# A gated decode block on one core: w_o's last part in 8 steps around the last value block, and the joining of one head's output moved into the middle of that block's products

## Chip, cores and metric

The kernel runs on one core of one Trainium2 chip. The metric is device microseconds (us) of one execution, and the figure compared is the median of several executions. One execution was also taken by the hardware profiler; its trace gives the span from the first to the last instruction and every duration used below.

## What is computed

Two rows of 448 numbers, `x`, are normalised, passed through attention against a cache of 4096 keys for 2 batches and 8 key/value heads of width 256 (two query heads share each), projected back by `w_o`, multiplied by a gate and added to `x`. The gate is a bilinear feed-forward block under a SiLU. All is float32.

```python
xn = _layernorm(x)
q = (xn @ wq).reshape(B, 1, 16, 256)
scores = einsum("bhqd,bhkd->bhqk", q, k) * 256 ** -0.5
o = einsum("bhqk,bhkd->bhqd", softmax(scores), v)
s = o.reshape(B, 1, 4096) @ wo          # wo: 4096 x 448
g = silu(((xn @ w_gate) * (xn @ w_up)) @ w_down)
return x + s * g
```

## The kernel before: tiling, stages and what sets their order

Nearly all the work is reading: keys and values are 16 blocks each (8 heads by 2 batches) of 128 partitions by 8192 floats (4096 KB by the profile), and every weight is laid out in the same shape. All these tiles come through one pool, `ring`, of five buffers. The function `plan` (line 51) writes the order of the transfers by hand, and `issue` (line 54) hands the next one to SyncE's DMA queue (SPq in the profile); a transfer may be cut by columns into several DMAs, so that its first part can be used before its last has landed. A transfer waits until the last reader of the tile five places earlier in that order is done.

The order of the last transfers (lines 76 to 81) is: the second part of `w_o` ("wo1", 10 steps), the keys of block 14, the keys of block 15, the values of block 14, the values of block 15 (four DMAs of 4096, 2048, 1024 and 1024 columns) and the last part of `w_o` ("wo2", 6 steps, as three DMAs of 3, 2 and 1 steps). A **step** of `w_o` is one of its 32 slices of 128 rows by 448 columns, 224 KB. Four steps belong to each head; steps 28 to 31 are the last head's.

The program is scheduled by hand: each engine runs its instructions in the order of the code.

- `scores` (line 194) makes 16 matmuls of keys against the queries (line 204) and two row maxima on VectorE (DVE, line 205).
- `softmax` (line 209) joins the maxima through small matmuls (lines 212 and 217), takes the exponentials on ScalarE (ACT, line 223), transposes them (line 225) and sums them (line 228).
- `values` (line 232) makes 16 matmuls with the values (line 238), accumulating in a PSUM bank `o` of which there is one, and then evacuates it through ScalarE into `ob`, with the softmax's division (line 240). The 16 products of one block use its columns in order, 512 each.
- `combine` (line 242) joins the pieces of a block's output by 8 small matmuls (line 248) in bank `cb`; `turn` (line 257) transposes the result on VectorE (line 258) into the form in which it meets `w_o`.
- `project` (line 263) multiplies steps of `w_o` at full width into bank `wide`; `spread` (line 161) moves that bank through ScalarE into bank `acc` (lines 164 and 166), and `project_last` (line 269) adds the remaining steps straight into `acc`, four matmuls of 112 columns each (line 272).

Blocks 0 to 13 run one after the other (lines 281 to 304), each with its scores, softmax and values. Then the outputs of six of them are joined, 10 steps of `w_o` are projected and spread, the scores and softmax of blocks 14 and 15 run, and then comes the tail that the change rewrites (lines 316 to 326): values of 14, joining of 14, values of 15, steps 26 and 27, joining of 15, steps 28 to 31. At the end two VectorE instructions multiply by the gate and add `x` (lines 330 and 331) and SyncE writes the result (line 332).

Of the kernel before, what the change touches and what calls it, by code (L numbers as in the profile page):

```python
# [9 lines left out]
AF = mybir.ActivationFunctionType  # L10
# [3 lines left out]
B, D = 2, 448  # L14
HKV, REP, SK, DH = 8, 2, 4096, 256
# [6 lines left out]
KB = 16  # L22
ROW = 8192
SL = D // NT
NC = HKV * 4
EARLY = 16
LATE = 26
EPS = 1e-5


# [5 lines left out]
def gated_decode_block(ctx: ExitStack, tc: tile.TileContext, x, xo, kt, v, wq, wo, wg, wu, wd, out):  # L36
    nc = tc.nc
# [6 lines left out]
    def bank(name="s", bufs=3):  # L44
        return psum.tile([128, 512], F32, name=name, bufs=bufs)
# [5 lines left out]
    def plan(name, src, cuts=None):  # L51
        todo.append((name, src, cuts or [0, src.shape[1]]))

    def issue(n=1):
        for name, src, cuts in todo[:n]:
            t = loaded[name] = ring.tile([128, ROW], F32, name="ring", align_bytes=512)
            for lo, hi in zip(cuts, cuts[1:]):
                nc.sync.dma_start(t[:, lo:hi], src[:, lo:hi])
        del todo[:n]

    N = HKV * B
    LAST = N - B
    plan("wq0", wq[0])
    for i in range(LAST):
# [10 lines left out]
        plan(f"v{i}", v[i % B, i // B])  # L75
    plan("wo1", wo[:, EARLY * D:LATE * D])
    plan(f"k{LAST}", kt[0, HKV - 1])
    plan(f"k{LAST + 1}", kt[1, HKV - 1])
    plan(f"v{LAST}", v[0, HKV - 1])
    plan(f"v{LAST + 1}", v[1, HKV - 1], [0, 4096, 6144, 7168, 8192])  # L80
    plan("wo2", wo[:, LATE * D:], [0, 3 * D, 5 * D, 6 * D])
    issue(5)

    x2 = const.tile([B, D], F32)
# [65 lines left out]
    def query(h):  # L150
        ps = bank()
        rows(ps, loaded[f"wq{h}"], 512)
        for r in range(REP):
            nc.vector.transpose(qT[h][:, :, :, :, r, :].rearrange("p b g d j -> p (g d) b j"),  # L154
                                ps[:, r * 256:(r + 1) * 256])
# [13 lines left out]
    def ffn_in():  # L169
        pp = []  # L170
        for w in ("wg", "wu"):
            ps = bank()
            rows(ps, loaded[w], FC)
            pp.append(ps)
        g = work.tile([128, FC], F32, name="h")
        nc.scalar.copy(g, pp[0][:, :FC])
        h = work.tile([128, FC], F32, name="h")
        nc.vector.tensor_mul(h, pp[1][:, :FC], g)
        nc.vector.transpose(hT.rearrange("p i m -> p (i m)"), h)

    def ffn_out():
        ps = bank()
        for i in range(14):
            t = i % NT
            nc.tensor.matmul(ps[W * t:W * (t + 1), :D], hT[:, i], loaded["wd"][:, i * D:(i + 1) * D],  # L185
                             start=i < NT, stop=i >= 14 - NT)
        y = bank()
        spread(ps, y, True, True)
        e = const.tile([128, SL], F32)
        nc.scalar.activation(e, y[:, :SL], AF.Sigmoid)  # L190
        nc.vector.tensor_mul(gate, y[:, :SL], e)


    def scores(i):
        g, b = divmod(i, B)
        k = loaded[f"k{i}"].rearrange("p (h d c n) -> p h d c n", h=2, d=2, c=NT)
        q = qT[g // 4][:, b, g % 4].rearrange("p d r j -> p d (r j)")
        m = work.tile([128, 4], F32, name="m")
        ss = []
        for h in range(2):  # L200
            s = bank()
            for d in range(2):
                for c in range(NT):
                    nc.tensor.matmul(s[W * c:W * (c + 1), :], q[:, d], k[:, h, d, c, :], start=d == 0, stop=d == 1)  # L204
            nc.vector.tensor_reduce(m[:, h:h + 1], s, axis=AX.X, op=OP.max)  # L205
            ss.append(s)
        return ss, m

    def softmax(ss, m):
        nc.vector.tensor_max(m[:, 2:3], m[:, 0:1], m[:, 1:2])  # L210
        sm = bank("sm", 1)
        nc.tensor.transpose(sm[:1, :128], m[:, 2:3], ident)  # L212
        mx = work.tile([1, NT, W], F32, name="mx")
        nc.vector.tensor_reduce(  # L214
            mx, sm[:1, None, :128].rearrange("p o (c j) -> p o j c", c=NT).to_broadcast([1, NT, W, NT]),
            axis=AX.X, op=OP.max)
        nc.tensor.matmul(sm[:, 128:129], mx.rearrange("p c j -> p (c j)"), one, start=True, stop=True)  # L217
        nc.vector.tensor_scalar(m[:, 3:4], sm[:, 128:129], -1.0 / 16, None, op0=OP.mult)  # L218
        su = work.tile([128, 4], F32, name="su")
        pT = []  # L220
        for h in range(2):
            p = work.tile([128, 512], F32, name="p")
            nc.scalar.activation(p, ss[h], AF.Exp, bias=m[:, 3:4], scale=1.0 / 16, accum_out=su[:, h:h + 1])  # L223
            t = work.tile([128, KB, W], F32, name="pT", bufs=4)
            nc.vector.transpose(t.rearrange("p i m -> p (i m)"), p)  # L225
            pT.append(t)
        nc.vector.tensor_add(su[:, 2:3], su[:, 0:1], su[:, 1:2])  # L227
        nc.tensor.matmul(sm[:, 130:131], add_head.rearrange("p a r j -> p (a r j)"), su[:, 2:3], start=True, stop=True)  # L228
        nc.vector.reciprocal(su[:, 3:4], sm[:, 130:131])
        return pT, su[:, 3:4]  # L230

    def values(i, pT, ob):

        pT, r = pT
        o = bank("o", 1)
        for e in range(KB):
            h, t, at = e // 8, e % NT, e % 8 * 2 * W
            nc.tensor.matmul(o[W * t:W * (t + 1), :], pT[h].rearrange("p i m -> p (i m)")[:, at:at + 2 * W:2],  # L238
                             loaded[f"v{i}"][:, e * 512:(e + 1) * 512], start=e < NT, stop=e >= KB - NT)
        nc.scalar.activation(ob, o, AF.Copy, scale=r)  # L240

    def combine(ob, n):

        cb = bank("cb", 1)
        src = ob.rearrange("p s (e d c k) -> p s e d c k", e=2, d=2, c=NT)
        for e in range(2):
            for c in range(NT):
                nc.tensor.matmul(cb[W * c:W * (c + 1), :n * 64], add_blocks[:, e].rearrange("p r j -> p (r j)"),  # L248
                                 src[:, :n, e, :, c, :], start=e == 0, stop=e == 1)
        return cb  # L250


    wide = bank("wide", 1)
# [3 lines left out]
    def turn(oT, cb, g, b, n):  # L257
        nc.vector.transpose(oT[:, g:g + n, :, :, DUP * b:DUP * (b + 1)].rearrange("p g d r j -> p (g d) r j"), cb)  # L258

    def heads(oT, i, first):  # L260
        return oT[:, i // 4 - first, i % 2, i % 4 // 2]

    def project(oT, first, lo, hi, name, base):
        for i in range(lo, hi):
            t = i % NT
            nc.tensor.matmul(wide[W * t:W * (t + 1), :D], heads(oT, i, first),  # L266
                             loaded[name][:, (i - base) * D:(i - base + 1) * D], start=i < NT, stop=i >= LATE - NT)

    def project_last(oT, first, i):
        for n in range(NT):  # L270
            at = (i - LATE) * D + n * SL
            nc.tensor.matmul(acc[W * n:W * (n + 1), :SL], heads(oT, i, first), loaded["wo2"][:, at:at + SL],  # L272
                             start=False, stop=i == NC - 1)

    query(0)
    issue()
    ob = work.tile([128, 8, 512], F32, name="ob", bufs=1)
    oT0 = const.tile([128, 4, 2, REP, W], F32)
    oT1 = const.tile([128, 3, 2, REP, W], F32)
    oT2 = const.tile([128, 1, 2, REP, W], F32)  # L280
    for i in range(LAST):
        g, b = divmod(i, B)
        ss = scores(i)
        issue()
        p = softmax(*ss)
        values(i, p, ob[:, b * 4 + g if g < 4 else b * 3 + g - 4])
        issue()
        if i == 1:
            ffn_in()
            issue(2)  # L290
        if i == 2:
            ffn_out()
            issue()
        if i == 5:
            query(1)
            issue()
        if i == 7:
            cb = combine(ob, 8)
            for n in range(B):
                turn(oT0, cb[:, n * 256:(n + 1) * 256], 0, n, 4)  # L300
            ob = work.tile([128, 8, 512], F32, name="ob", bufs=1)
        if i == 8:
            project(oT0, 0, 0, EARLY, "wo0", 0)
            issue()
    cb = combine(ob, 6)
    for n in range(B):
        turn(oT1, cb[:, n * 192:(n + 1) * 192], 0, n, 3)
    project(oT1, 4, EARLY, LATE, "wo1", EARLY)
    issue()
    spread(wide, acc, True, False)  # L310
    ps = []
    for i in range(LAST, N):
        ss = scores(i)
        issue()
        ps.append(softmax(*ss))
    for i in range(LAST, N):
        b = i - LAST
        values(i, ps[b], ob[:, 6 + b])
        issue()
        if b == B - 1:  # L320
            for n in range(LATE, NC - 4):
                project_last(oT1, 4, n)
        cb = combine(ob[:, 6 + b:], 1)
        turn(oT2, cb[:, :64], 0, b, 1)
    for i in range(NC - 4, NC):
        project_last(oT2, 7, i)

    r0 = const.tile([128, SL], F32)
    r1 = const.tile([128, SL], F32)
# [40 lines left out]
```

## Time and profile before

| what | value |
|---|---|
| median of 3 runs | 380.46 us (379.8 to 380.95) |
| profiled execution | 379.4 us, of which the span is 377.3 us |
| TensorE matmul (PE) | busy 221.4 us, 59% |
| TensorE weight load (PEld) | busy 64.9 us, 17% |
| VectorE / ScalarE | busy 72.7 us / 39.8 us |
| bytes moved by DMA | 158.75 MB, mean 421 GB/s |
| mean granted TensorE clock | 0.78 of full |

How to read it: the span is cut into stages with different limits, so the busy shares of the whole do not tell what the end waits for. Three views matter here. The chain of waits follows the last instruction back to what released it. The windows view gives, for any stretch, how long each engine was busy, which share of the TensorE clock was granted (PEclk) and what the DMA engines moved. The list of DMA issues gives, for each transfer, its size and the time from issue to landing. A matmul of this kernel appears as two records in the trace, so the 16 matmuls of `values` are 32 records, and one step in `project_last` is 8.

### The profile page before, as it was taken

What the parts mean: (1) busy time and instruction counts of PE and PEld (TensorE: products, weight loads), DVE (VectorE), ACT (ScalarE), POOL (GpSimd) and SP (SyncE); (2) the same over time, 40 slices, a digit from 0 to 9 for tenths busy, and PEclk for the clock granted to TensorE, in tenths of its full rate; (3) what the DMA queues carried; (4) which work ended last, traced back from release to release, by engine and by line L of the source; (5) the groups of instructions that cost most, each with busy time, mean ns of one, the idle gap of its engine ahead of it and who ended that gap; (6) DMA issues with size and microseconds to landing.
All of it is one profiled execution on the core that took longest, in us unless ns stands there. A gap on an engine that the chain in (4) does not pass through costs nothing.

```text
span 377.3 us, 3373 instructions
## 1 busy us (share of the span) xinstructions
PE 221.4 (59%) x1444; PEld 64.9 (17%) x1444; DVE 72.7 (19%) x176; ACT 39.8 (11%) x87; POOL 1.2 (0%) x7
## 2 busy tenths in 40 slices
PE   0665565667365556546566655664656476575765
PEld 0112121112111211101122111121112121111122
DVE  3013120121021402102121310213021210304211
ACT  1001011002202100100102100021002010111020
POOL 1000000000000000000000000000000000000000
PEclk9966968666966878887876877669786966699668
DMA  8999999999999999999999999999999999999992
GB/s 338 437 434 419 431 438 434 419 438 449 427 419 438 438 436 431 423 434 441 433 424 429 433 442 438 417 436 434 440 424 431 438 429 445 424 432 436 410 419 94
DMA packets 6530, 158.75 MB, mean 421 GB/s; under 512 B 754, under 2 KB 884, under 8 KB 1396
## 3 DMA queue, kind: packets, MB, share of 16 engines
q1 hardware_dynamic: 6496, 158.54, 97.8%
q8 instruction: 11, 0.18, 0.2%
q14 instruction: 3, 0.02, 0.0%
q10 hardware_dynamic: 20, 0.01, 0.0%
HBM read 158.54 MB, written 0.00 MB: 420 GB/s over the span
## 4 chain that ended last, share of the span: by engine, by line
DMA 72%; PE 21%; DVE 4%; issue 1%; ACT 1%; SPq 0%; ACTq 0%
DMA ring<-kt 60%; DMA ring<-v 12%; PE s L204 10%; PE o L238 8%; DVE pT L225 1%; PE s L185 1%; PE cb L248 1%; DVE m L205 1%; DVE mx L214 1%; PE sm L228 1%; ACT ob L240 1%; PE sm L217 0%; ACT p L223 0%; PE sm L212 0%; PE acc L272 0%
## 5 line engine op out<-in xcount | busy, mean ns | idle before, releaser
L204 PE MATMUL s<-ring,qT 128*32 128x512 f32 x512 | 80.6, 786 | 51.2 <-DMA ring<-kt 51.1
L238 PE MATMUL o<-ring,pT 128*32 128x512 f32 x512 | 85.5, 830 | 2.0 <-DMA ring<-v 2.0
L205 DVE TENSOR_REDUCE m<-s 128x1 f32<-128x512 f32 x32 | 22.1, 692 | 175.4 <-PE s L204 175.4
L223 ACT ACTIVATE p<-s,m 128x512 f32<-128x512 f32 x32 | 21.7, 682 | 196.8 <-DVE m L218 196.7
L204 PEld LDWEIGHTS s<-ring,qT 128*32 128x32 f32 x512 | 20.1, 138 | 109.6 <-issue 78.3
L228 PE MATMUL sm<-su,add_head 128*128 128x1 f32 x32 | 9.1, 353 | 42.5 <-DVE su L227 42.5
L238 PEld LDWEIGHTS o<-ring,pT 128*32 128x32 f32 x512 | 20.1, 147 | 52.9 <-issue 52.4
L225 DVE STREAM_TRANSPOSE pT<-p 128x512 f32<-128x512 f32 x32 | 22.1, 711 | 15.7 <-ACT p L223 15.7
L142 PE MATMUL s<-ring,xnT 128*32 128x512 f32 (+1 forms) x96 | 14.9, 772 | 13.2 <-DMA ring<-wq 8.4
L240 ACT ACTIVATE ob<-o,su 128x512 f32<-128x512 f32 x16 | 11.0, 687 | 109.4 <-PE o L238 109.4
L228 PEld LDWEIGHTS sm<-su,add_head 128*128 128x128 f32 x32 | 7.7, 300 | 43.8 <-DVE su L227 43.8
L212 PE MATMUL sm<-ident,m 128*1 128x128 f32 x16 | 4.3, 269 | 17.3 <-DVE m L210 17.3
L217 PE MATMUL sm<-one,mx 1*128 1x1 f32 x32 | 6.5, 270 | 12.4 <-DVE mx L214 12.4
L214 DVE TENSOR_REDUCE mx<-sm 1x128 f32<-1x512 f32 x16 | 10.9, 679 | 7.0 <-PE sm L212 7.0
L266 PE MATMUL wide<-ring,oT 128*32 128x448 f32 x52 | 7.4, 686 | 4.1 <-DMA ring<-wo 3.4
L217 PEld LDWEIGHTS sm<-one,mx 1*128 1x128 f32 x32 | 5.1, 199 | 15.8 <-DVE mx L214 15.8
L142 PEld LDWEIGHTS s<-ring,xnT 128*32 128x32 f32 x96 | 3.6, 137 | 23.0 <-issue 18.1
L258 DVE STREAM_TRANSPOSE oT<-cb 128x256 f32<-128x256 f32 (+2 forms) x6 | 1.9, 346 | 26.5 <-PE cb L248 26.5
L212 PEld LDWEIGHTS sm<-ident,m 128*1 128x1 f32 x16 | 1.3, 79 | 32.0 <-issue 26.1
L223 ACT ACTIVATION_READ_ACCUMULATOR p<-s,m 128x1 f32 x32 | 6.3, 196 | 0.0
L248 PE MATMUL cb<-ob,add_blocks 128*32 128x64 f32 (+2 forms) x64 | 4.3, 385 | 2.9 <-ACT ob L240 2.9
L154 DVE STREAM_TRANSPOSE qT<-s 128x256 f32<-128x256 f32 x4 | 1.6, 428 | 22.3 <-PE s L145 22.3
(53 smaller groups left out, 40.3 us busy)
## 6 DMA issues: line engine op xcount, KB each, us to landing
ring<-kt SPq DMA_DIRECT2D x16, 4096.0 KB, 40.7
ring<-v SPq DMA_DIRECT2D x15, 4096.0 KB, 41.9
ring<-wq SPq DMA_DIRECT2D x2, 3584.0 KB, 11.4
ring<-wo SPq DMA_DIRECT2D x1, 3584.0 KB, 40.8
ring<-wg SPq DMA_DIRECT2D x1, 3136.0 KB
ring<-wu SPq DMA_DIRECT2D x1, 3136.0 KB
ring<-wd SPq DMA_DIRECT2D x1, 3136.0 KB, 35.1
ring<-wo SPq DMA_DIRECT2D x1, 2240.0 KB, 37.9
```

Source lines behind the costliest of these rows:

```text
L142: nc.tensor.matmul(ps[W * c:W * (c + 1), :n], xnT[:, k, :], block(NT * k + c), start=k == 0, stop=False)
L204: nc.tensor.matmul(s[W * c:W * (c + 1), :], q[:, d], k[:, h, d, c, :], start=d == 0, stop=d == 1)
L205: nc.vector.tensor_reduce(m[:, h:h + 1], s, axis=AX.X, op=OP.max)
L214: nc.vector.tensor_reduce(mx, sm[:1, None, :128].rearrange("p o (c j) -> p o j c", c=NT).to_broadcast([1, NT, W, NT]), axis=AX.X, op=OP.max)
L217: nc.tensor.matmul(sm[:, 128:129], mx.rearrange("p c j -> p (c j)"), one, start=True, stop=True)
L223: nc.scalar.activation(p, ss[h], AF.Exp, bias=m[:, 3:4], scale=1.0 / 16, accum_out=su[:, h:h + 1])
L225: nc.vector.transpose(t.rearrange("p i m -> p (i m)"), p)
L228: nc.tensor.matmul(sm[:, 130:131], add_head.rearrange("p a r j -> p (a r j)"), su[:, 2:3], start=True, stop=True)
L238: nc.tensor.matmul(o[W * t:W * (t + 1), :], pT[h].rearrange("p i m -> p (i m)")[:, at:at + 2 * W:2], loaded[f"v{i}"][:, e * 512:(e + 1) * ...
L240: nc.scalar.activation(ob, o, AF.Copy, scale=r)
L248: nc.tensor.matmul(cb[W * c:W * (c + 1), :n * 64], add_blocks[:, e].rearrange("p r j -> p (r j)"), src[:, :n, e, :, c, :], start=e == 0, s ...
L266: nc.tensor.matmul(wide[W * t:W * (t + 1), :D], heads(oT, i, first), loaded[name][:, (i - base) * D:(i - base + 1) * D], start=i < NT, sto ...
```

## The change

The second part of `w_o` has 8 steps instead of 10 and the last part 8 instead of 6. The last part is laid out in memory in another order, 24, 25, 28, 29, 30, 31, 26, 27, and fetched by four DMAs of 2, 4, 1 and 1 steps. The values of block 15 come in three DMAs (4096, 3072 and 1024 columns) instead of four. Block 15's products are accumulated in bank `wide`, which `spread` has emptied by then, instead of in `o`. The first 8 of them stand ahead of the joining of block 14, the other 8 behind it. Step 24 stands where steps 26 and 27 stood (ahead of the joining of 15), step 25 behind that joining, then steps 28 to 31, and steps 26 and 27 last.

```diff
-LATE = 26
+LATE = 24
+THIRD = [24, 25, 28, 29, 30, 31, 26, 27]
...
-    plan(f"v{LAST + 1}", v[1, HKV - 1], [0, 4096, 6144, 7168, 8192])
-    plan("wo2", wo[:, LATE * D:], [0, 3 * D, 5 * D, 6 * D])
+    plan(f"v{LAST + 1}", v[1, HKV - 1], [0, 4096, 7168, 8192])
+    plan("wo2", wo[:, LATE * D:], [0, 2 * D, 6 * D, 7 * D, 8 * D])
...
-    def values(i, pT, ob):
-
-        pT, r = pT
-        o = bank("o", 1)
-        for e in range(KB):
+    def values(i, pT, o, lo=0, hi=KB):
+
+        for e in range(lo, hi):
...
-        nc.scalar.activation(ob, o, AF.Copy, scale=r)
...
     def project_last(oT, first, i):
         for n in range(NT):
-            at = (i - LATE) * D + n * SL
+            at = THIRD.index(i) * D + n * SL
             nc.tensor.matmul(acc[W * n:W * (n + 1), :SL], heads(oT, i, first), loaded["wo2"][:, at:at + SL],
-                             start=False, stop=i == NC - 1)
+                             start=False, stop=i == THIRD[-1])
...
-        values(i, p, ob[:, b * 4 + g if g < 4 else b * 3 + g - 4])
+        o = bank("o", 1)
+        values(i, p[0], o)
+        nc.scalar.activation(ob[:, b * 4 + g if g < 4 else b * 3 + g - 4], o, AF.Copy, scale=p[1])
...
-    for i in range(LAST, N):
-        b = i - LAST
-        values(i, ps[b], ob[:, 6 + b])
-        issue()
-        if b == B - 1:
-            for n in range(LATE, NC - 4):
-                project_last(oT1, 4, n)
-        cb = combine(ob[:, 6 + b:], 1)
-        turn(oT2, cb[:, :64], 0, b, 1)
-    for i in range(NC - 4, NC):
+
+    o = bank("o", 1)
+    values(LAST, ps[0][0], o)
+    nc.scalar.activation(ob[:, 6], o, AF.Copy, scale=ps[0][1])
+    issue()
+    o = bank("wide", 1)
+    values(LAST + 1, ps[1][0], o, 0, KB // 2)
+    cb = combine(ob[:, 6:], 1)
+    turn(oT2, cb[:, :64], 0, 0, 1)
+    values(LAST + 1, ps[1][0], o, KB // 2, KB)
+    nc.scalar.activation(ob[:, 7], o, AF.Copy, scale=ps[1][1])
+    project_last(oT1, 4, 24)
+    cb = combine(ob[:, 7:], 1)
+    turn(oT2, cb[:, :64], 0, 1, 1)
+    project_last(oT1, 4, 25)
+    for i in range(28, 32):
         project_last(oT2, 7, i)
+    for i in range(26, 28):
+        project_last(oT1, 4, i)
...
-    wo = c(np.asarray(A_wo).reshape(NC, 128, D).transpose(1, 0, 2)).reshape(128, NC * D)
+    wo = np.asarray(A_wo).reshape(NC, 128, D)[[*range(LATE), *THIRD]]
+    wo = c(wo.transpose(1, 0, 2)).reshape(128, NC * D)
```

## The prediction

> **What bounds the kernel now.** I read the DMA row of the page first, then the chain of waits backwards from the end, then the windows view of the tail, then the DMA issues.
>
> ```profile
> DMA  8999999999999999999999999999999999999992
> DMA 72%; PE 21%; DVE 4%; issue 1%; ACT 1%; SPq 0%; ACTq 0%
> ```
>
> The DMA engines are full until the last of 40 slices. No edit changes the bytes, so everything up to the last landings stays, and only the tail can move. The chain's last pieces (start, us, what):
>
> ```profile
> 311.12 38.42 DMA ring<-kt
> ...
> 349.59 6.19 PE s L204 x32
> ...
> 361.46 5.34 PE o L238 x32
> ...
> 366.83 0.70 ACT ob L240
> ...
> 367.57 0.43 PE cb L248 x16
> 368.00 3.48 PE o L238 x32
> ...
> 371.50 0.70 ACT ob L240
> ...
> 372.24 0.47 PE cb L248 x16
> ...
> 372.74 0.26 DVE oT L258
> ...
> 373.04 1.02 PE acc L272 x32
> ```
>
> So behind the landing of block 15's keys at 349.55 nothing waits for a transfer any more: TensorE and what it hands to ScalarE and VectorE set the end. The last steps of `w_o`, by the DMA issues (KB, us to landing):
>
> ```profile
> ring<-wo SPq DMA_DIRECT2D x1, 448.0 KB, 32.1
> ring<-wo SPq DMA_DIRECT2D x1, 224.0 KB, 22.6
> ```
>
> The timeline has the last of them issued at 349.56, so it landed at 372.2; the last 1024 columns of V (issued 333.85, 35.1 us) landed at 368.95. The six steps took 3.25 us, 0.54 each. The final 32 records start 0.84 us after the last landing: that, and the 1.02 us of those records, is all the room there is in front of the transfers.
>
> TensorE's clock decides the pace. In windows of 3.41 us (PE busy, records, PEclk, DMA share, GB/s):
>
> ```profile
> 351.25:354.67 3.42, 3.42 (x20) 0.50 0.89 383
> 354.67:358.08 3.41, 1.53 (x15) 1.00 1.01 432
> 358.08:361.49 3.41, 0.83 (x8) 0.50 0.93 399
> 361.49:364.91 3.42, 3.42 (x20) 0.50 1.00 420
> 364.91:368.32 3.41, 2.59 (x44) 1.00 1.02 419
> ```
>
> The granted clock is 1.00 or 0.50 and changes only at multiples of 3.41 us from one another, all through the trace. Half became full after a window busy 3.13 us, not after one of 2.97; full became half after 1.53, not after 1.65. A record of 512 columns takes 0.107 us of pace at full clock and 0.213 at half (rows of four: 0.43 and 0.85).
>
> **The change, part by part.**
>
> *Two steps later in the queue.* 2 x 0.54 = 1.08 us of transfer move behind the last V, so both last keys and values land 1.08 earlier; block 15's keys at 348.47. TensorE can use it: the project ahead has 16 records instead of 20 (2.45 us down to 1.96), so scores of 14 start about 1.0 earlier, and that block's last small matmul ends at 347.87 (before 348.87), ahead of the keys. Block 15's values land whole at 367.87 and, at 0.54 us per 224 KB, their first 2048 KB at 362.9; block 14's, 4096 KB or 9.9 us ahead of that, by 358.1. None is late below.
>
> What the 1.08 brings depends on the window grid. **On the profiled grid**: scores of 15 run at half clock to 354.67. Before, (354.67 - 349.59) / 0.213 = 23.8 of 32 records, and 8.2 x 0.107 = 0.88 behind; now 28.9, and 0.33 behind: 0.55 earlier, half of the shift. The softmax chain is fixed. Values of 14 start at 360.9, at half clock to 364.91: 18.8 records, then 13.2 x 0.107 = 1.41 instead of 1.69. Of 1.08, **0.28** is left. **Over all positions of the grid** nothing is lost: work and grid shifted together give the same durations, so the mean gain is about 1.0 to 1.08.
>
> *Half of the last V's products ahead of the joining of 14.* Before, TensorE idles 0.82 us at 366.75 (its idle time before L248), waiting for ScalarE's 0.70 evacuation. Now 16 records (1.71 us at full clock) stand there in another bank: **-0.82**. Queued behind the joining are the other 16 products, which need ScalarE at 367.5, long done at 368.2. If block 15's values were late, the cover would go and 0.82 come back; the first half lands 3 us ahead. The joining itself (0.24 us until the next products start) stays.
>
> *Order of the steps.* Step 24 (8 records, about 0.25) hides under the evacuation of 15 (0.70), where 26 and 27 were hidden; step 25 under the transpose (0.26). Behind the transpose stand 48 records instead of 32: 1.02 x 1.5 = 1.53, **+0.51**. What is queued behind step 24 is the joining of 15; its step lands at 367.87 + 1.08 = 368.95 and is asked for at 370.2. Steps 28 to 31 land by 371.1, 26 at 371.7, 27 at 372.2 again.
>
> *DMAs.* V has one piece less, w_o one more; SP still issues seven in the same order, all over 20 us before their landing, past waits that end about 1 us earlier. DVE's and ACT's orders hold as many instructions as before. I price this at nothing, with 0.1 either way; the cover is the queue's backlog.
>
> **Sum.** On the profiled grid -0.28 - 0.82 + 0.51 = -0.59: the accumulation ends at 373.5 instead of 374.06, 1.3 behind the last landing, and what follows (two VectorE instructions, the write) stays. 379.4 becomes 378.8. With the shift in full: -1.04 - 0.82 + 0.51 = -1.35. The floor is the last landing and one step, 372.20 + 0.25 + about 0.2 (a record of `acc` lasts 0.26 us at a pace of 0.03): 372.65, 1.41 below the profiled end.
>
> Which grid do the runs have? The three lie 0.4 to 1.55 us above the profiled one, though the transfers are the same; a step to full clock that comes 1 us later costs 0.5 us in each of the two stages above, so 1 or 2 us give that much. On the profiled grid block 14's products meet the change to full 3.5 us after their start, and since a window must be busy 3.13 us, hardly a grid is kinder to that stage. So the typical run has a later step and gains more than 0.59. The Trainium skill, "TensorE: Matmul & The Clock Gate", "Part 1: The HAM clock gate", says that the activity window is 3413 ns, free-running, and is not reset when a kernel starts. The trace agrees with 3.41 us, and that the grid's place differs by execution one profile cannot show; by that rule the sum would be -1.35, with a fixed grid -0.59.
>
> I take -1.25, the full shift less a little that the floor takes where TensorE is early anyway. From the median: 380.46 - 1.25 = **379.2 us**. A measurement of this kernel can tell about 0.3%, 1.14 us, from no change.
>
> **Rivals.**
>
> 1. *The grid is the same in every execution.* For it: one profile, one grid. Against it: runs that spread over 1.15 us. Then -0.59: 379.9. Chance 0.25.
> 2. *The floor is reached in the typical run.* If a window that was just not busy enough (347.84 to 351.25 holds 2.25 us; with work 1.08 earlier about 2.9 of the needed 3.13) counts, the clock rises one window earlier, and the end falls to the last landing. From a median run 1.06 above the profiled one that is -(1.06 + 1.41) = -2.5: 378.0. For: how close 2.9 is to 3.13. Against: it needs it in most grids. Chance 0.15.
> 3. *Nothing is there to gain.* Where the clock rises early in both kernels, both end at the floor, and the 0.51 behind the transpose is paid without the 0.82 saved: 0 to +0.2, 380.6. For: then products of 15 wait for V in both. Against: the chain shows no such wait. Chance 0.12.
> 4. *Slower: TensorE overtakes the transfers and loses its clock.* Place: the window in which the last products wait for V. Products of a block need 3.45 us at full clock and its values 9.7 us to land, so a TensorE that has caught up is busy 35% of the time, under the 1.65 of 3.41 (48%) that kept the clock. Then the 48 last records run at half: between nothing and 1.53 more, with the last products and the joining another 0.7. From the profiled end -0.59 + 2.2 = +1.6; 382.1 from the median. It decides when the window around 368.3 to 371.7 holds under 1.65 us of work; on the profiled grid it holds over 2.5 in the new order (8 products, the joining, a step), so I give it 0.08.
>
> **Numbers.** The forecast has 0.40. Faster by over 0.3% means under 379.3: most of rival 2, a bit over half of the forecast's spread and a little of rival 1: 0.47. Within: the rest of those two and rival 3: 0.45. Slower: rival 4 in full, 0.08. The range leaves out rival 4 and the outer halves of 2 and 3: 378.0 to 380.5.
>
> **What would show it.** Block 15's keys landing near 348.5; no idle of 0.8 us before the first small joining; the last 48 records starting about 1 us before the old 373.0 and ending at 372.7 to 373.5; the last landing within 0.2 us of 372.2. I am wrong if TensorE waits for a landing of `w_o` ahead of the joining of 15, if PEclk is 0.50 behind 368, or if the last landing moves.

## The result and the profile after

| | median | runs |
|---|---|---|
| before | 380.57 us | 379.8 to 381.35, 6 runs |
| changed | 378.26 us | 377.87 to 378.55, 6 runs |

The ratio is 0.994, 95% interval 0.9924 to 0.9956: 2.3 us faster, by 1.7 to 2.9. The forecast was 1.25 us faster, 379.2: the time lies inside the forecast's range, but 1.25 lies outside this interval. A second measurement (e6 below) gave 0.9958, 0.9942 to 0.9975, which is 1.6 us, by 1.0 to 2.2. The changed kernel's runs lie within 0.7 us of one another; those of before, over all measurements here, from 378.73 to 381.54. The profiled execution of the changed kernel, 378.55 us with a span of 376.4, is the slowest of its six; that of before, 379.4, was faster than all six of its runs.

The page: the DMA engines are as full as before, and their part of the chain grew from 72% to 76% while TensorE's fell from 21% to 18%.

```profile
DMA  8999999999999999999999999999999999999993
DMA 76%; PE 18%; DVE 3%; issue 1%; ACT 1%; SPq 0%; ACTq 0%
```

The chain's end in the changed kernel (start, us, what), to be laid beside the one in the prediction:

```profile
311.03 37.77 DMA ring<-kt
...
348.84 6.54 PE s L205 x32
...
361.02 5.49 PE o L237 x32
366.50 1.72 PE wide L237 x16
368.22 0.22 PE cb L246 x16
368.44 1.77 PE wide L237 x16
...
370.24 0.69 ACT ob L326
...
370.98 0.47 PE cb L246 x16
...
371.48 0.26 DVE oT L256
...
371.78 1.40 PE acc L270 x48
```

ScalarE's evacuation of block 14, which stood between the two blocks' products at 366.83, is gone from the chain: the first 16 records of block 15 stand in its place, and the joining follows without a gap. Block 15's keys land at 348.80 (before 349.55), its products end 1.3 us earlier, the accumulation ends at 373.18 (before 374.06). The last landing is at 372.57 (issued 348.81, 23.8 us), before 372.2.

The window grid of this profile is almost that of before (PE busy, records, PEclk, DMA share, GB/s; the first line is from the profile of before, the others from this one):

```profile
347.84:351.25 3.41, 2.25 (x10) 0.50 1.02 442
...
347.80:351.21 3.41, 2.95 (x14) 0.50 0.94 404
351.21:354.62 3.41, 3.41 (x20) 0.50 1.01 437
...
361.45:364.86 3.41, 3.41 (x20) 0.50 1.00 421
364.86:368.28 3.42, 3.42 (x52) 1.00 1.01 418
```

So the two profiles can be laid on one another: both rise to full clock at 354.6 and at 364.9. On this one grid the accumulation ended 0.88 us earlier, of which 0.85 shows in the time (379.4 to 378.55). The rest of the 2.3 lies in where the two profiled executions stand among the runs: that of before 1.17 us below its median, that of the changed kernel 0.29 above.

### The profile page after: what moved, and what is told of

It is laid out like the page before. It is cut to its first block, busy times and chain, and to the rows that moved or that the text cites. A ratio compares the mean times of both kernels' runs of the same rounds, so it can differ in the third digit from the quotient of the medians.

```text
span 376.4 us, 3397 instructions
## 1 busy us (share of the span) xinstructions
PE 222.5 (59%) x1456; PEld 65.6 (17%) x1456; DVE 72.7 (19%) x176; ACT 39.8 (11%) x87; POOL 1.2 (0%) x7
## 4 chain that ended last, share of the span: by engine, by line
DMA 76%; PE 18%; DVE 3%; issue 1%; ACT 1%; SPq 0%; ACTq 0%
DMA ring<-kt 55%; DMA ring<-v 12%; DMA ring<-wd 9%; PE s L205 8%; PE o L237 6%; DVE pT L226 1%; PE wide L237 1%; PE s L186 1%; PE cb L246 1%; DVE m L206 1%; DVE mx L215 1%; PE sm L229 0%; PE acc L270 0%; SPq L59 0%; PE sm L218 0%
## 5 line engine op out<-in xcount | busy, mean ns | idle before, releaser
L205 PE MATMUL s<-ring,qT 128*32 128x512 f32 x512 | 82.0, 799 | 50.9 <-DMA ring<-kt 50.9
L237 PE MATMUL o<-ring,pT 128*32 128x512 f32 x480 | 82.4, 849 | 1.6 <-DMA ring<-v 1.6
L237 PEld LDWEIGHTS o<-ring,pT 128*32 128x32 f32 x480 | 18.9, 149 | 51.5 <-issue 50.9
L286 ACT ACTIVATE ob<-o,su 128x512 f32<-128x512 f32 x14 | 9.6, 687 | 98.8 <-PE o L237 98.8
L264 PE MATMUL wide<-ring,oT 128*32 128x448 f32 x48 | 6.6, 698 | 4.1 <-DMA ring<-wo 3.3
```

Source lines behind the costliest of these rows:

```text
L286: nc.scalar.activation(ob[:, b * 4 + g if g < 4 else b * 3 + g - 4], o, AF.Copy, scale=p[1])
```

## The experiments

All were compared with the kernel before on the same chip. "Theory A" is what I held after the first result: TensorE's chain behind block 15's keys sets the end, each part of the change takes time from it, and the places of the clock's steps make the spread.

**e1, the split alone.** The kernel before with the products of block 15 in bank `wide`, 8 on each side of the joining; nothing else.

```diff
...
+    o = bank("wide", 1)
+    values(LAST + 1, ps[1][0], o, 0, KB // 2)
+    cb = combine(ob[:, 6:], 1)
+    turn(oT2, cb[:, :64], 0, 0, 1)
+    values(LAST + 1, ps[1][0], o, KB // 2, KB)
...
```

> The kernel before with one part of the change: block 15's products go to the bank wide, 8 of them stand ahead of the joining of block 14 and 8 behind it; the transfers, their cuts and the order of w_o's steps are those of before. Theory A (the end is set by TensorE's chain behind the landing of block 15's keys, every part of the change takes time from that chain, and the place of the clock's steps adds the spread): the 0.8 us of idle ahead of the first small joining is gone, nothing is added behind the transpose, so about 0.8 below before, 379.6 to 379.9, and a spread over 1 us as before. Rival B (the two steps moved behind the last V are all of the gain): within 0.3 of before. Rival C (the idle is all of it): within 0.4 of the changed kernel, 378.3 to 378.7.

Measured: 379.61 against 380.21; ratio 0.9985, 0.9968 to 1.0003, so 0.6 us, between 1.2 and nothing: A's size, but not clear of zero. Runs from 378.24 to 380.83. The profiled one was the slowest, and its timeline shows why (start, us, records, idle time before and what ended it):

```profile
340.50 5.20 PE L204 MATMUL s<-ring,qT 128*32 128x512 f32 x32 [2.00 <-DMA ring<-kt]
...
350.81 0.59 PE L228 MATMUL sm<-su,add_head 128*128 128x1 f32 x2 [2.58 <-DVE su L227]
351.33 1.08 PE L204 MATMUL s<-ring,qT 128*32 128x512 f32 x4
```

On this grid the project of `w_o` had run at full clock, TensorE then waited 2.00 us for block 14's keys, and the window 336.87 to 340.28 held only 1.00 us of work. The clock fell, the scores of block **14** took 5.20 us instead of 3.64, its softmax ended at 351.4, and the keys of block 15, landed at 350.12, waited 1.2 us for TensorE. In the profile of before those scores met full clock:

```profile
339.55 3.64 PE L204 MATMUL s<-ring,qT 128*32 128x512 f32 x32 [0.52 <-DMA ring<-kt]
```

**e2, the split undone.** The changed kernel with all of block 15's products behind the joining of 14.

```diff
-    values(LAST + 1, ps[1][0], o, 0, KB // 2)
     cb = combine(ob[:, 6:], 1)
     turn(oT2, cb[:, :64], 0, 0, 1)
-    values(LAST + 1, ps[1][0], o, KB // 2, KB)
+    values(LAST + 1, ps[1][0], o)
```

> The changed kernel with the split undone: all 16 products of block 15 stand behind the joining of block 14 again; the transfers and the order of the steps are the changed ones. Theory A: the idle of 0.8 us comes back, so 0.7 to 0.9 above the changed kernel, 379.0 to 379.2, and the profile's accumulation ends about 1.4 us behind the last landing instead of 0.6. Rival B: as the changed kernel, 378.3. Rival C: as before, 380.5.

Measured: 378.81 against 380.21; 0.9962, 0.9948 to 0.9976, so 1.45 us faster than before, and 0.55 above the changed kernel's first median, where theory A had 0.7 to 0.9. The idle time is back in the timeline; the second line is that of the kernel before:

```profile
366.39 0.42 PE L246 MATMUL cb<-ob,add_blocks 128*32 128x64 f32 x15 [0.82 <-ACT ob L319]
...
367.57 0.43 PE L248 MATMUL cb<-ob,add_blocks 128*32 128x64 f32 x16 [0.82 <-ACT ob L240]
```

The accumulation ends 1.10 us behind the last landing (372.12), where theory A had about 1.4. Rival C (the split is all) does not hold: most of the gain is there without it. Rival B (the shift is all) is not excluded by the ratios, 0.9962 here against 0.994 and 0.9958 (e6) for the changed kernel, whose intervals overlap. Against it speaks that ten of e2's twelve runs lie above 378.55, the highest of the changed kernel's twelve, though those were measured apart from these.

**e3 and e4, both kernels with TensorE kept busy: a fill that was too big.** 17 extra matmuls in the gaps of each of the last two softmax chains; their result is read by nobody.

```diff
+    def warm(n):
+        d = bank("cb", 1)
+        for _ in range(n):
+            nc.tensor.matmul(d[:W, :D], add_tiles.rearrange("p b j -> p (b j)"),
+                             hT.rearrange("p i m -> p (i m)"), start=True, stop=True)
...
+        if fill[0]:
+            warm(fill[0])
         nc.tensor.transpose(sm[:1, :128], m[:, 2:3], ident)
...
-        ps.append(softmax(*ss))
+        ps.append(softmax(*ss, (4, 3, 10)))
```

> The changed kernel with 17 extra matmuls of 448 columns whose result nobody reads, in the gaps of each of the last two softmax chains (4, 3 and 10 ahead of their three small matmuls), which keep TensorE busy while it would wait. Theory A, with the clock as the cause of the spread: scores of block 15 and values of block 14 run at full clock on every place of the window grid, both end 2 to 3 us earlier, the end is left to the last landing, and all runs lie within 0.4 of 377.9. Rival D (a TensorE that overtakes the transfers loses its clock again in the last windows): PEclk 0.50 behind 365 us, the 48 last records up to 1.5 us longer, 378.3 to 379.5. Rival E (the clock is not what bounds): as the changed kernel, 378.3, with its spread of 0.7.

> The kernel before with the same 17 extra matmuls in the gaps of each of the last two softmax chains. Theory A: with the clock full TensorE is early enough in the old order too, so the end is left to the last landing and the change is worth under 0.4: 377.8 to 378.3, against 380.5 without the fill. Rival E (the clock is not what bounds): as before, 380.5. Between (order and clock both count): 378.6 to 379.6, with the idle ahead of the small joining still 0.8 us.

Measured: 390.67 and 391.86, ratios 1.0267 and 1.0315: 10 and 12 us slower, which none of the theories had. The error was the size of the fill:

```profile
348.49 7.70 PE L213 MATMUL cb<-hT,add_tiles 128*32 128x448 f32 x20
```

Twenty records of 448 columns took 7.70 us, 0.385 each, where 512 columns in `values` are paced at 0.107. All of the fill writes one group of 32 rows of the bank; the 16 matmuls of `values` go round four groups. So the fill held back both softmax chains by several us. The clock was full in every window, so these runs say what a fill costs and nothing on the theories.

**e6, the changed kernel again**, beside the next three on one chip.

> The changed kernel once more, for its spread and for another place of the window grid, beside the next three on one chip. Theory A (the shifted transfers let TensorE reach the last landing on nearly every grid): median 0.9 to 1.2 below the kernel with the split undone relative to the kernel before, that is 1.8 to 2.3 below before, and a spread under 1.2 us where before has over 2. Rival: the 2.3 of the first measurement was a matter of grids, then 0.6 to 1.2.

Measured: 378.14 (377.82 to 378.55) against 379.85 (379.12 to 380.87); 0.9958, 0.9942 to 0.9975. The 1.6 us fall between theory A (1.8 to 2.3) and its rival (0.6 to 1.2), and against e2's ratio the split brings 0.15 us here, where A had 0.9 to 1.2; only the small spread, 0.7, came as A said. The grid of this profile stands 0.3 us later than in the first, and on it TensorE was early. Block 15's keys landed at 348.32, the window behind them was nearly filled, and the clock rose at its end, one window earlier than the 354.6 of the first two profiles:

```profile
348.10:351.52 3.42, 3.15 (x16) 0.50 1.06 460
351.52:354.93 3.41, 2.29 (x21) 1.00 0.92 399
...
371.04 0.97 PE L270 MATMUL acc<-ring,oT 128*32 128x112 f32 x32 [0.18 <-DVE oT L256]
372.21 0.94 PE L270 MATMUL acc<-ring,oT 128*32 128x112 f32 x16 [0.20 <-DMA ring<-wo]
```

The four steps of the last head are done at 372.0, and then TensorE waits for `w_o`: step 26, and step 27, whose landing is at 372.7 (issued 348.34, 24.4 us). The accumulation ends 0.44 us behind that. This is the floor, and 378.55, the highest of these six runs, was its profile: the last landing was 0.5 later than in the trace of before.

**e7, the shift alone.** `w_o`'s steps in their natural order, no split; the last part has 8 steps. The lines are against the changed kernel; block 15's products stand as in e2.

```diff
-THIRD = [24, 25, 28, 29, 30, 31, 26, 27]
+THIRD = [24, 25, 26, 27, 28, 29, 30, 31]
...
-    plan("wo2", wo[:, LATE * D:], [0, 2 * D, 6 * D, 7 * D, 8 * D])
+    plan("wo2", wo[:, LATE * D:], [0, 4 * D, 6 * D, 7 * D, 8 * D])
...
-    project_last(oT1, 4, 24)
+    for i in range(24, 28):
+        project_last(oT1, 4, i)
```

> The shift alone: w_o's last part has 8 steps, in the natural order 24 to 31, fetched by DMAs of 4, 2, 1 and 1; steps 24 to 27 stand ahead of the joining of block 15 and 28 to 31 behind its transpose, as 26 and 27 and 28 to 31 did before; block 15's products are not split. Theory A as the prediction has it: -1.0 to -1.1 against before, 0.3 to 0.5 better than without the split but with the new order. Rival F (the shift is worth more than it moves, because on some grids block 14's scores also start at half clock and block 15's keys then wait for TensorE): -1.4 to -1.9. Rival G (the shift is lost at half clock as on the first profile's grid): -0.3.

Measured: 378.58 (377.99 to 380.35); 0.9968, 0.9954 to 0.9982, so 1.2 us below before, by 0.7 to 1.75. That is the prediction's full shift; rival G (0.3) is out, F (1.4 to 1.9) can't be told from it. Against e2, which has the new order besides, it is 0.2 us slower by the ratio, though 0.2 lower by the median: a cost of the new order is too small for these times to tell. In this profile too the clock rose one window early, after one that held 2.86 us:

```profile
347.99:351.40 3.41, 2.86 (x17) 0.50 0.99 423
351.40:354.81 3.41, 2.30 (x22) 1.00 0.95 408
```

**e8 and e9, the light fill.** 8 matmuls of 224 columns in each of the two chains, sized by e3 (the lines are against e3 and e4).

```diff
-            nc.tensor.matmul(d[:W, :D], add_tiles.rearrange("p b j -> p (b j)"),
-                             hT.rearrange("p i m -> p (i m)"), start=True, stop=True)
+            nc.tensor.matmul(d[:W, :D // 2], add_tiles.rearrange("p b j -> p (b j)"),
+                             hT[:, :7].rearrange("p i m -> p (i m)"), start=True, stop=True)
...
-        ps.append(softmax(*ss, (4, 3, 10)))
+        ps.append(softmax(*ss, (2, 1, 5)))
```

> The changed kernel with 8 extra matmuls of 224 columns, whose result nobody reads, in each of the last two softmax chains (2, 1 and 5 ahead of the three small matmuls), sized by the first fill: a record on one column group took 0.385 us for 448 columns at full clock, so these take 0.39 us each, 3.1 in all, and fit in gaps of 1.1, 0.8 and 2.6. Theory A: scores of 15 and values of 14 run at full clock, TensorE waits for V in the end; at the floor, 0 to 0.4 below the changed kernel. Rival D: PEclk 0.50 in the windows that hold the last products, which then wait for V; 0.3 to 1.5 above the changed kernel.

> The kernel before with the same 8 extra matmuls in each of the last two softmax chains. Theory A: with full clock behind block 15's keys, TensorE is early enough in the old order, and of the 2.3 us that the change brings 1.2 to 2.0 come without it: 1.2 to 2.0 below before, spread under 1.2 us. Rival E (clock does not matter there): as before, within 0.3. If scores of 14 meet half clock, the fill takes twice as long and delays that softmax by up to 1.7 us, which would show as single runs above before's.

Measured: the changed kernel with fill 377.98 (0.9958, 0.9941 to 0.9975), the kernel **before** with fill 378.11 (378.02 to 379.0; 0.9963, 0.995 to 0.9977), beside 378.14 for the changed kernel alone. So half clock is what made the kernel before late: with nothing of the change, extra work that keeps TensorE busy brings 1.4 us of the 1.6 that the change brought on this chip, and on top of the change it brings nothing that can be told. What spread is left in e9, 378.02 to 379.0, is partly the transfers': its profile is the highest run, and has the latest last landing of all profiles, 372.99, with the accumulation ending 0.58 us behind it. The windows of e9:

```profile
347.80:351.21 3.41, 2.21 (x17) 1.00 1.02 442
351.21:354.62 3.41, 3.41 (x32) 1.00 0.91 394
...
361.45:364.86 3.41, 2.60 (x40) 1.00 0.97 399
364.86:368.28 3.42, 2.94 (x26) 1.00 1.01 416
```

PEclk is 1.00 where both profiles had 0.50. Now the old order waits for transfers:

```profile
367.28 1.07 PE L250 MATMUL o<-ring,pT 128*32 128x512 f32 x8 [0.41 <-DMA ring<-v]
368.50 1.05 PE L250 MATMUL o<-ring,pT 128*32 128x512 f32 x4 [0.16 <-DMA ring<-v]
369.81 1.05 PE L250 MATMUL o<-ring,pT 128*32 128x512 f32 x4 [0.25 <-DMA ring<-v]
```

Rival D, a TensorE that overtakes the transfers and loses its clock, did not come: no window of e9 behind 347.8 and ahead of the end holds less than 2.19 us of work, and in e8 the thinnest but the last, 363.05 to 366.47, holds 1.94 and is followed by full clock.

**e10, the order of the steps undone**, split and shift kept (e7's edit in the changed kernel).

> The changed kernel with the order of w_o's steps undone: the last part in the natural order 24 to 31, fetched by DMAs of 4, 2, 1 and 1; steps 24 to 27 ahead of the joining of block 15, 28 to 31 behind its transpose. The shift of two steps and the split stay. If the two steps more behind the transpose cost what the prediction said (0.51 us), this is 0.3 to 0.5 faster than the changed kernel, 2.2 or more below before. If they run in time that would be spent waiting for the last landing, it is as the changed kernel, within 0.2: 1.6 to 2.1 below before.

Measured: 378.24 (377.94 to 378.69); 0.9955, 0.9938 to 0.9972. As the changed kernel; the interval, 1.1 to 2.4 us, does not exclude by itself the 2.2 that a cost of 0.51 would have meant. The trace shows why none is seen. With 32 records behind the transpose instead of 48, the end is still 0.44 us behind the last landing (372.36): they start at 371.79, because steps 24 to 27 now stand ahead of the joining and wait for `w_o` themselves:

```profile
370.22 0.97 PE L270 MATMUL acc<-ring,oT 128*32 128x112 f32 x32 [0.56 <-DMA ring<-wo]
...
371.79 1.01 PE L270 MATMUL acc<-ring,oT 128*32 128x112 f32 x32 [0.37 <-DVE oT L256]
```

**e11 and e12, the light fill in one chain of the kernel before.**

```diff
-        ps.append(softmax(*ss, (2, 1, 5)))
+        ps.append(softmax(*ss, (2, 1, 5) if i == LAST else (0, 0, 0)))
```

(e12 has `i > LAST`.)

> The kernel before with the light fill (2, 1 and 5 extra matmuls of 224 columns, results unread) in the softmax chain of block 14 alone. It keeps the clock full for the scores of block 15, and not for the values of block 14. If both stages count alike: half of what the fill in both chains brought (1.4 to 1.7), 0.6 to 1.0 below before. If the values' stage is what counts, within 0.3 of before.

> The kernel before with the light fill in the softmax chain of block 15 alone. The scores of block 15 keep their usual clock; the values of block 14 meet full clock if the scores before them reached it. If both stages count alike: 0.6 to 1.0 below before. If the scores' stage is what counts, within 0.3 of before.

Measured: 378.28 (0.9956, 0.9941 to 0.9971) and 378.48 (0.9961, 0.9947 to 0.9975) against 379.9. Either fill alone brings 1.5 to 1.7 us, all that both bring. I had expected halves. In e12 the scores of 15 took 5.97 us and the values of 14 took 3.64, after which TensorE waited for V; the accumulation ended 0.58 us behind the last landing. In e11 the scores of 15 ran in 3.64 us, and the values of 14 at half clock still took 6.10, but started 1.0 us earlier than in the first profile of before. That profile is the highest of e11's ten runs, 379.14, and ends 1.74 us behind the last landing, so it does not show how the median of 378.28 came about. What it shows is block 14's scores at half clock, ahead of any fill, as in e1:

```profile
339.69 6.21 PE L204 MATMUL s<-ring,qT 128*32 128x512 f32 x32 [3.20 <-DMA ring<-kt]
```

Block 15's keys, landed at 349.31, waited for TensorE until 351.22. By the medians, one stage at full clock is enough to bring TensorE close to the floor, and the second finds little left.

**e13, the kernel before, one look.**

> The kernel before once more, one look, for the place of its window grid. A grid that is free of the kernel's start stands elsewhere than 330.77 plus multiples of 3.41 us, and block 14's products meet the change to full clock at another time than 3.5 us after their start. A grid that starts with the kernel stands within 0.1 of it.

Measured: 379.76 us. Its clock changes at 331.37, 348.43, 355.26, 358.67 and 365.50, 0.6 us later than in the first profile. Block 14's products started at 361.51 and met full clock 4.0 us later, not 3.5, and the accumulation ended 0.35 us later though the keys of 15 had landed 0.25 earlier (349.30). Over the 14 profiles of this case the grid's place in its 3.41 us reaches over 2.7 us, from 328.7 (e3) to 331.4. So it is not tied to the kernel's start. It is not spread evenly either: twelve of the 14 lie from 330.0 to 331.4.

## Why the prediction was right or wrong, point by point

- **What bounds the kernel**: right. Behind block 15's keys TensorE's chain set the end in both profiles, and the transfers stayed as they were. The last landing came 0.37 us later, 372.57 for 372.2, where the prediction allowed 0.2; executions differ by more than that (372.0 to 373.0 over all profiles). Counted from each profile's own last landing, the accumulation ended 1.82 us behind it in the first profile of before and 2.42 in e13; 1.10 in e2 and 0.65 in e7; and 0.57, 0.44 and 0.44 where shift and split are both in (the result, e6, e10).
- **Two steps later in the queue**: right in mechanism, and in size as far as it can be told. On the profiled grid, with keys 0.75 us earlier in that execution, the products of 14 ended 0.30 earlier, where the working had 0.28 for 1.08. Counted from the last landing the keys came 22.65 us ahead in both profiles of before and 23.8 in the changed one, 1.1 more, as worked out. Over the runs e7 measured 1.2 (0.7 to 1.75) for 1.04. That agreement is looser than it looks: the working took every place of the grid as equally likely, which the 14 profiles do not bear out. What the working did not see is block 14: on grids such as e1's and e11's its scores too meet half clock, and then it is TensorE that keeps block 15's keys waiting. Part of the shift's worth may lie there; I have two profiles of it and did not measure its share.
- **Half of the products ahead of the joining**: right in the trace. The idle 0.82 us is gone from the chain, and comes back in e2's timeline. In the times it is not clear of nothing: 0.6 alone (nothing to 1.2), and on top of the shift 0.15 (e2 against e6) to 0.85 (e2 against the result) by the ratios.
- **Order of the steps, +0.51**: this is the term that failed. On the profiled grid the 48 records took 1.40 us instead of 1.02, +0.38; in the times, e10 against e6 and e7 against e2 show no cost, though their intervals are too wide to exclude one of 0.5. The two steps run where TensorE would otherwise wait for the last landing (e6: idle until 372.21 for `w_o`), and e10 without them ends as far behind it as e6. The prediction put them on the path of the typical run and set the floor apart as a limit; after -0.82 and -1.04 the typical run is at the floor, and there 0.51 is not paid. Away from it some cost may stay: without the split, e2's profile ends 1.10 us behind its last landing, e7's 0.65. With the term at nothing the sum is -1.86, between the two measurements, 1.6 and 2.3; since the gain stops at the floor, that fit proves little.
- **DMAs at nothing**: right; the cover held in every profile, where the last of these DMAs was issued more than 22 us ahead of its landing.
- **Which grid the runs have**: right in direction, and it decided the size. The choice of -1.25 over the -0.59 of the profiled grid rested on the spread of three runs; e9 showed that the clock is the larger part of that spread (378.02 to 379.0, beside 379.12 to 380.87 for before), e13 that the grid moves. The Trainium skill, "TensorE: Matmul & The Clock Gate", "Part 1: The HAM clock gate", whose window is free-running, agrees with that. Its table has the clock fall after an idle window; here windows with up to 1.64 us of work in 3.41 were followed by half clock (profile of the kernel before), and the measurement decides.
- **Rivals**: the grid that is the same in every execution (379.9) fell with e13. The floor in the typical run (378.0, chance 0.15) is the nearest to what came: 378.26 and 378.14. In part it came by the way that rival gave, the clock rising one window earlier: so it did in e2, e6 and e7, after windows that held 3.18, 3.15 and 2.86 us. In the result's own profile the window 347.80 to 351.21 held 2.95 and was not enough, nor was 2.58 in e10. (The working's 2.9 is 2.8 by its own times, since block 14's small matmul leaves the window; the keys came later than it had them.) So of five profiles with the shift and no fill three rose early: two of these windows were over the needed 3.13, and the third shows that this figure, read off one trace, was not sharp. Nothing to gain (380.6) could fit only such runs of before as 378.73, which may have been at the floor anyway; they have no trace. The slower case did not occur, as e8 and e9 show.
- **The number**: 379.2 is 0.9 us too high, and the range held the result near its lower end. The parts were mostly right and their sum was too small: it charged 0.51 that was not paid, and gave little weight to the early rise of the clock. How much of the gap each of the two makes was not measured.

## What to carry to other kernels

When a profile's end hangs on an engine whose clock changes with its load, one profile is one draw: lay the clock's windows over the tail, ask how the sum comes out on other places of that grid, and look at the spread of the runs before choosing. A cheap filling of the engine's gaps is the experiment that tells lateness by clock from lateness by order; size it by a record of the same shape first. And a cost that falls behind the last landing's wait is no cost: when several gains add up to the floor, price the remaining terms at the floor, not on the old path. A threshold read off one trace may not be sharp, so a rival that misses it by a little deserves more than a small chance.

## What was not expected of the hardware

- 448 columns on one group of 32 rows took 0.385 us per record at full clock (e3), 512 columns going round four groups 0.107. At the first rate 512 columns would take 0.44, four times 0.107, which fits four matmuls side by side in `values`.
- The load that raises the clock is not as sharp as the first profile made it: a half-clock window with 2.86 us of busy time was followed by full clock in e7, and one with 3.11 was not in e6. Busy time in the records tells it only roughly.
- A wait of 2.00 us ahead of block 14's scores (e1) was followed by half clock, in which they took 5.20 us instead of 3.64 and kept block 15's keys waiting for 1.2.
